# Rows of the FFT input in partition blocks of 32 and 20 instead of 8 and 4

## The chip, the cores and the metric

The kernel runs on one core of one Trainium2 chip. A core has a matrix engine (PE, with its weight loads shown as PEld), three engines for elementwise work (DVE, ACT, POOL), an engine that here only issues transfers (SP), and 16 DMA engines that carry the transfers which SP, ACT and POOL issue. The metric is device time in microseconds of one execution; several runs are summed up by their median.

## The reference

The input x has 8 batches of 3008 rows and 256 columns in float32. The kernel computes the real part of a two-dimensional Fourier transform of each batch and feeds the result, row by row, to a gated feed-forward block of width 1536:

```python
X = np.fft.fft(x, axis=1)
X = np.fft.fft(X, axis=2)
h = X.real.reshape(8 * 3008, 256)
g = h @ w_gate
silu = g * (1.0 / (1.0 + np.exp(-g)))
out = (silu * (h @ w_val)) @ w_out
```

## The kernel before, in words

**How the work is laid out.** The transform along a batch's 3008 rows is done with symmetries. Rows are taken in four quarters of R = 752. Pairs of neighbouring rows that rise from the start of each quarter (the code calls them up, one transfer reads all four quarters of some pairs) are added to pairs that fall from each quarter's end (down, one transfer for each quarter). Of the 188 pair positions of a quarter, 128 go to the tile XA, one to a partition, and the other 60 to half of the tile XC, where two batches share the 128 partitions. POOL folds these rows (lines 171 to 197: cross, even, odd, ab, ce, bb) into bf16 coefficients, PE multiplies the coefficients by cosine and sine tables (lines 1368 to 1419), DVE writes the result into the tiles Pt and Qt, and from there on the feed-forward block runs over 24 tiles of about 512 columns, each column standing for two output rows.

**Units.** A tile is worked through in 12 units of 128 hidden channels; the kernel has 288 units. A unit multiplies Pt and Qt by weights Wp, Wq and Wm into the PSUM tiles g and v (line 972). ACT and DVE turn them into silu values and products (lines 1045 to 1186), POOL multiplies the mirrored ones (line 1183), and PE multiplies hp and hm by Wo (line 1236). The table KINDS gives each unit one hexadecimal digit, which says which engine does which step; a digit with bit 1 set saves one matmul and costs two DVE instructions.

**What sets the order.** From the first unit on nothing is issued directly. Every step is recorded by S.add with an engine, an assumed duration, an assumed latency, and a due time (PE's recorded time so far plus SHIFT and BIAS of the tile). S.run then plays the program through and fixes the order on each queue. The loads are recorded in run_loads (line 1297) with an assumed issue time us, a latency lat and a time ring that the transfer holds the DMA queue. The waiting rows for the next tile are recorded at unit 6 of a tile (first_rows16, line 1569) and unit 7 (all_rows, line 1577): the first copies row 0 of Qt to the tile br, the second copies br to all partitions of bc, both on SP's queue. Stores of finished rows (line 1249) are also on SP's queue. SP uses eight completion semaphores in turn, so the ninth transfer waits until the first has landed.

**What stands in front of the units.** Lines 252 to 652 are issued in the order in which they are written. They load batch 0 directly: one transfer for all 128 rising pairs (line 258), four falling ones by fall_a (line 261, 256 KB each, two from ACT's queue and two from SP's), one for the rising pairs of XC0 (line 264), four by fall_c (line 267, 120 KB each). PE places the rising rows in the partition order of the falling ones with the permutations putA and putC (line 435), DVE adds rising and falling rows (lines 444 to 457), and the first Pt, Qt and weights follow. The first unit's first matmul on line 972 starts at 18.86 us. Batch 1 comes next: load_c(1) partly in front of the units (the first C1_EARLY of its transfers) and partly in the planned part, load_a(1) at unit A1_LOAD.

**Blocks.** [...] A rising transfer (up_block) carries one block, all four quarters. A falling transfer (down_set) carries one quarter of all the blocks; its source has the dimensions [blocks, pairs of a block, 512 elements]. m_cols (line 313) works out a partition's row from LA or LC, so tables follow the blocks.

Of the kernel before, what the change touches and what calls it, by code (L numbers as in the profile page):

```python
# [19 lines left out]
def kernel(  # L20
# [8 lines left out]
    nc = tc.nc  # L29
    B, M, D = x.shape  # L30
    Dff = moe_w_gate.shape[1]
    P = 128
# [20 lines left out]
    NCR = GH - P  # L53
# [62 lines left out]
    rrO = XA.rearrange("p a q d -> p (a q d)")[:, 4 * T:4 * T + 4 * GH].rearrange("p (c q n) -> p c q n", c=2, q=2)  # L116
    kfO = EOf.rearrange("p e a d -> p (e a d)")[:, 4 * (P + 1):4 * (P + 1) + GH]

    LA, NA = 8, P // 8
    LC, NC_ = 4, NCR // 4  # L120

    def up_block(b, j, n):
        return rows_at(b, 2 * j - 1, [[2 * D, n], [R * D, 4], [1, 2 * D]])
# [4 lines left out]
    def down_set(b, a, j, L, n):  # L128

        return rows_at(b, R * (a + 1) - 2 * j, [[2 * L * D, n], [-2 * D, L], [1, 2 * D]])  # L130

    JA, JC = P - LA + 1, GH - LC + 1

    C1_EARLY = 6
    C1_ORDER = "uuduuduuduuduumuueuueuece"
    A1_ORDER = "uuuuduuuuduuuuduuuud"

    def load_a(b, q):
        X3 = XA.rearrange("p a q d -> p a (q d)")
        res = ([lambda h=h: q.dma_start(out=X3[LA * h:LA * (h + 1), 0:4, :],  # L140
                                         in_=up_block(b, JA - LA * h, LA)) for h in range(NA)] +
                [lambda a=a: q.dma_start(out=X3[:, 4 + a, :], in_=down_set(b, a, JA, LA, NA)) for a in range(4)])
        return in_order(A1_ORDER, u=res[:NA], d=res[NA:]) if b == 1 else res

    def in_order(order, **todo):
        todo = {k: list(v) for k, v in todo.items()}
        return [todo[k].pop(0) for k in order]

    def load_c(b, q):

        X3 = XC.rearrange("p a q d -> p a (q d)")
        p0 = 64 * (b % 2)
        pm = p0 + NCR
        r = slice(p0, p0 + NCR)
        ups = [lambda h=h: q.dma_start(out=X3[p0 + LC * h:p0 + LC * (h + 1), 0:4, :],
                                       in_=up_block(b, JC - LC * h, LC)) for h in range(NC_)]
        mid = [lambda: q.dma_start(out=XC[pm:pm + 1, 0:4, 1],
                                   in_=rows_at(b, 0, [[R * D, 1], [R * D, 4], [1, D]]))]
        if b != 1:
            return ups + [lambda a=a: q.dma_start(out=X3[r, 4 + a, :], in_=down_set(b, a, JC, LC, NC_))  # L160
                          for a in range(4)] + mid

        def down(a, k):
            q.dma_start(out=XC[0:NCR, 4 + a, 0] if k else XC[r, 4 + a, 0],
                        in_=rows_at(b, R * (a + 1) - 2 * JC + k, [[2 * LC * D, NC_], [-2 * D, LC], [1, D]]))

        downs = [[lambda a=a, k=k: down(a, k) for a in range(4)] for k in range(2)]
        return in_order(C1_ORDER, u=ups, d=downs[0], e=downs[1], m=mid,
                        c=[lambda: q.dma_start(out=XC[0:NCR, 0:4, 1], in_=XC[r, 0:4, 0])])
# [377 lines left out]
    loads_c1 = load_c(1, q)  # L547
    for load in loads_c1[:C1_EARLY]:
        load()
# [133 lines left out]
    def rows(r0, n, step):  # L683
# [5 lines left out]
    C1_AT = 12  # L689
    A1_AT = 20  # L690
    C2_AT = 39
    A1_LOAD = 8
    ROW_1 = 12
    ROW_2 = 24
    ROW_3 = 35
# [46 lines left out]
    )  # L742
    BIAS = {(t, k): v for t, row in enumerate(BIAS_ROWS) for k, v in zip(SHIFT, row)}
    ES_BUFS = 2
# [175 lines left out]
    def pool_us(n):  # L920
# [6 lines left out]
    ROW_PE = {ROW_1: 1, ROW_2: 2, ROW_3: 3}  # L927
    KINDS = (
        "wwwwwwwwwwww",
        "06ww20001013",  # L930
        "031303160011",
        "000010312133",
        "010210112012",
        "10110b103133",
        "001601031052",
        "300171700001",
        "331213005030",
        "010271031001",
        "34130b310300",
        "01b300700101",  # L940
        "21312101b300",
        "001371310011",
        "32120011b212",
        "10130b135030",
        "000135003170",
        "033170001011",
        "213b21011200",
        "103b10319610",
        "4030b13300b0",
        "616404563200",  # L950
        "143034169230",
        "706150233313",
    )

    def whole(u):
# [328 lines left out]
    lo = C2_AT  # L1284
    for b in range(2, B, 2):
        u = slot[(b, 0)] - 1
        spread(("C", b), 12, lo, (lo + u) // 2)
        spread(("A", b), 12, (lo + u) // 2 + 1, u)
        lo = min(u + 26, slot[(b + 1, 0)] - 2)
# [5 lines left out]
    loads = []  # L1295

    def run_loads(n):
        for what, k, fn in loads[:n]:
            up = k < (NA if what[0] == "A" else NC_)
            r, w, us, ring = [], [((what[0],), k)], 0.4 if up else 0.62, 0.57 if up or what[0] == "C" else 1.14  # L1300
            if what == ("A", 1):
                r = [(("C",), C1_ORDER.rindex("u"))]
                us, ring = (0.42, 0.75) if A1_ORDER[k] == "u" else (0.75, 1.1)
            if what == ("C", 1):
                us, ring = (0.48, 0.75) if C1_ORDER[k] == "u" else (0.95, 1.0)
                if C1_ORDER[k] == "c":
                    r = [(("C",), j) for j, o in enumerate(C1_ORDER) if o == "u"]
            S.add("SP", us, fn, r=r, w=w, after=[(("A",), "pre" if A1_ORDER[k] == "d" else "preW")] if what == ("A", 1) else [],
                  lat=2.5, ring=ring)
        del loads[:n]  # L1310

    FOLD = (("X", "F"), ("F", "E"), ("F", "O"), ("EO", "A"), ("A", "CE"), ("EO", "BB"))
# [112 lines left out]
    for b, part in jobs[1:]:  # L1425
        for eo in range(2):
            u = slot[(b, part)] + eo
# [149 lines left out]
    def all_rows(t):  # L1577
        w = row_width(t)

        def fn():  # L1580
            bc[t] = bcp.tile([P, T], BF16, name="bc")
            nc.sync.dma_start(out=bc[t][:, :w], in_=T_["br", t][0:P:8, :w].unsqueeze(1).to_broadcast([16, 8, w]))
        return fn

    def row_op(t):
        w = width(t)
        kr = (("g", ("bc", t)), 0)

        def product():
            T_[kr] = psG.tile([P, T], F32, name="g")  # L1590
            nc.tensor.matmul(T_[kr][:, :w], sel, pq_tiles(t)[1][:, :w], start=True, stop=True)

        def copy():
            bc[t] = bcp.tile([P, T], BF16, name="bc")
            nc.scalar.copy(bc[t][:, :w], T_[kr][:, :w])  # L1595

        S.add("PE", pe_us(w), product, r=[(("pq", t), "Q")], w=[kr], new=[kr[0]])
        S.add("ACT", act_us(w), copy, r=[kr], w=[(("bc", t), 0)], new=[("bc", t)])
# [4 lines left out]
    S.hold("st", 0)  # L1603
    for k in range(C1_EARLY):
        S.add("DMA", 0.01, lambda: None, w=[(("C",), k)], lat=2.0)
# [11 lines left out]
    for i, u in enumerate(units):  # L1617
        t, f = u
        S.tile = t
        for op in before.pop(i, ()):  # L1620
            op()
        if i == 1:
            loads.extend((("C", 1), k, fn) for k, fn in enumerate(loads_c1) if k >= C1_EARLY)
        if i == A1_LOAD:
            loads[0:0] = ((("A", 1), k, fn) for k, fn in enumerate(load_a(1, nc.sync)))
        run_loads(LOADS if i < 20 else LOADS_LATER)
        if i in ROW_PE:
            row_op(ROW_PE[i])
        for j, k in enumerate((i - ROW_GAP, i)[::-1]):
            tr, fr = divmod(k, nF)  # L1630
            if k >= 0 and fr == 6 and 2 < tr < nT - 1:
                if j:
                    S.add("SP", 0.55, all_rows(tr + 1), r=[(("br", tr + 1), 0)], w=[(("bc", tr + 1), 0)], new=[("bc", tr + 1)], lat=4.5, shift="ROW")
                else:
                    S.add("SP", 0.55, first_rows16(tr + 1), r=[(("pq", tr + 1), "Q")], w=[(("br", tr + 1), 0)], new=[("br", tr + 1)], lat=3.6, shift="ROW")
        if i == RESCALE:
            state["scaled"] = True
            S.add("ACT", 1.3, lambda: nc.scalar.activation(Wm[:, 1], Wm[:, 1], AF.Copy, scale=-0.5),
                  r=[(("Wm",), (fc, 1)) for fc in range(3)], w=[(("Wm",), 1)])
        if i == 2:  # L1640
            S.add("POOL", 1.06, lambda: nc.gpsimd.dma_start(out=Wo, in_=moe_w_out.rearrange("(f p) d -> p f d", p=P)),
                  w=[(("Wo",), 0)], lat=12.0)
        part_a(u)
        if owork:
            owork.run(4)
        if i + 1 < len(units) and seeded(units[i + 1]):
            seed_op(units[i + 1])
        if prev is not None:
            part_b(prev)
            if prev[1] == nF - 1:  # L1650
                owork = OWork(prev[0])
            if owork:
                owork.run(4)
        for what, j in fold_at.get(i, ()):
            fold_step(what, j, i)
        for what in act_at.pop(i, ()):
            load_next(what)
        if i in spread_at:
            spread_op(spread_at[i])
        if i in job_at:  # L1660
            transform_op(*job_at[i])
        prev = u
# [35 lines left out]
```

## Time and profile before

Three runs took 598.28, 599.33 and 600.06 us. The profiled execution took 600.4 us, of which the page's span, from the first to the last instruction, is 598.6 us; its granted clock is 0.999.

| engine | busy us | share of the span |
|---|---|---|
| PE | 587.0 | 98% |
| DVE | 570.3 | 95% |
| ACT | 557.4 | 93% |
| POOL | 527.8 | 88% |

The loads of x by kind, from the list of DMA issues: 30 falling XA transfers of 256 KB and 112 rising ones of 64 KB on SP's queue, 28 falling XC transfers of 120 KB and 105 rising ones of 32 KB, 8 falling half ones of 60 KB for batch 1, two falling XA transfers on ACT's queue, and the two large rising transfers of batch 0.

A time of the span that PE stands idle is lost only if nothing later gives it back; other engines' idle time costs nothing by itself. A window of the profile gives each engine's busy time in a stretch, the share of the 16 DMA engines that was busy (1.00 is all sixteen; transfers that overlap on an engine can lift it a little above), and the rate that they moved.

### The profile page before, as it was taken

Reading aid. Unit: us, or ns where it says so; the run is one execution under the profiler, and the core shown is the slowest. Engines: PE = TensorE matmul, PEld = TensorE weight load, DVE = VectorE, ACT = ScalarE, POOL = GpSimd, SP = SyncE. Lnnn points to the kernel's source line nnn. Section 1 sums busy time; section 2 is a strip of 40 time slices with the busy share of each in tenths; the row PEclk is TensorE's granted clock in tenths of the full one; section 3 lists DMA queues with packets and bytes.
Section 4 is the critical chain, followed back from the end, with each engine's and each line's share of the span. In section 5 each row is a group of like instructions: output and inputs, shape, how many; then the busy total and the mean of one; then the engine's idle time right before and its main releaser. Section 6 shows DMA issues by size and latency. Waiting matters only on the chain.

```text
span 598.6 us, 12468 instructions
## 1 busy us (share of the span) xinstructions
PE 587.0 (98%) x3953; PEld 389.2 (65%) x4012; DVE 570.3 (95%) x1064; ACT 557.4 (93%) x1080; POOL 527.8 (88%) x486
## 2 busy tenths in 40 slices
PE   7999999999999999999999999999999999999997
PEld 5456666666666666666666666666666666666686
DVE  8989999999999999999999999999999999999993
ACT  8778989989998999999999999999999999999995
POOL 8977999999899999998999998897986868687772
PEclk9999999999999999999999999999999999999999
DMA  9956347454715523454127122046221202111212
GB/s 247 150 110 115 109 121 141 132 140 117 178 46 107 136 70 113 123 129 138 57 55 166 46 62 82 19 115 161 63 64 37 65 19 80 48 46 53 60 54 81
DMA packets 51082, 57.65 MB, mean 96 GB/s; under 512 B 7283, under 2 KB 38439, under 8 KB 51017
## 3 DMA queue, kind: packets, MB, share of 16 engines
q1 hardware_dynamic: 47433, 53.91, 35.2%
q0 software_dynamic: 3216, 2.36, 2.8%
q8 instruction: 31, 0.51, 0.4%
q10 hardware_dynamic: 368, 0.59, 0.3%
q14 instruction: 34, 0.28, 0.2%
HBM read 29.43 MB, written 24.65 MB: 90 GB/s over the span
## 4 chain that ended last, share of the span: by engine, by line
PE 71%; ACT 8%; DMA 6%; DVE 4%; POOL 3%; issue 3%; SPq 1%; ACTq 0%; POOLq 0%; DVEq 0%
PE o L1236 30%; PE g L972 19%; PE v L972 16%; DMA XA<-in_x_dram 5%; ACT sv L1159 2%; PE o L1394 2%; PE g L1394 2%; ACT v L1045 2%; ACT es L1107 1%; POOL hm L1183 1%; DVE sv L1175 1%; ACT sp L1084 1%; DVE hp L1186 1%; ACT sp L1156 1%; ACT ev L1243 1%
## 5 line engine op out<-in xcount | busy, mean ns | idle before, releaser
L1183 POOL TENSOR_TENSOR hm<-sv 128x1024 bf16<-128x1024 f32 (+2 forms) x137 | 254.7, 1862 | 44.1 <-ACT sv L1159 17.7
L1175 DVE SCALAR_TENSOR_TENSOR sv<-es,v 128x512 f32<-128x512 f32 (+2 forms) x262 | 173.6, 668 | 5.4 <-PE v L972 2.8
L1236 PE MATMUL o<-Wo,hm 128*128 128x256 bf16 (+1 forms) x1128 | 163.6, 273 | 0.3
L1236 PE MATMUL o<-Wo,hp 128*128 128x256 bf16 (+1 forms) x1104 | 159.7, 273 | 0.2
L1186 DVE TENSOR_TENSOR hp<-sp,v 128x512 bf16<-128x512 f32 (+2 forms) x233 | 154.2, 668 | 2.8 <-PE v L972 2.0
L1236 PEld LDWEIGHTS <-hm 128*128 128x128 bf16 (+2 forms) x1140 | 111.8, 98 | 57.9 <-issue 2.5
L1236 PEld LDWEIGHTS <-hp 128*128 128x128 bf16 (+2 forms) x1140 | 111.9, 98 | 55.8 <-issue 0.9
L1159 ACT ACTIVATE sv<-g 128x512 f32<-128x512 f32 (+2 forms) x179 | 116.7, 671 | 4.6 <-PE g L972 2.3
L1084 ACT ACTIVATE sp<-g 128x512 f32<-128x512 f32 (+2 forms) x179 | 110.5, 621 | 4.1 <-PE g L972 2.7
L972 PE MATMUL v<-Pt,Wp 128*128 128x512 bf16 (+2 forms) x288 | 105.4, 375 | 1.8 <-DVE hp L1186 0.5
L972 PE MATMUL g<-Pt,Wp 128*128 128x512 bf16 (+2 forms) x280 | 104.4, 374 | 0.9 <-ACT sv L1159 0.7
L1045 ACT ACTIVATE v<-bc,w 128x512 f32<-128x512 bf16 (+2 forms) x146 | 104.6, 717 | 0.4
L1109 DVE SCALAR_TENSOR_TENSOR es<-bc,w,v 128x512 f32<-128x512 bf16 (+2 forms) x128 | 92.6, 731 | 2.4 <-ACT bc L1595 0.8
L1107 ACT ACTIVATE es<-v 128x512 f32<-128x512 f32 (+2 forms) x146 | 90.0, 618 | 3.8 <-PE g L972 1.0
L972 PE MATMUL g<-Qt,Wq 128*128 128x512 bf16 (+2 forms) x247 | 90.5, 374 | 0.4
L972 PEld LDWEIGHTS <-Wp 128*128 128x128 bf16 x576 | 56.3, 98 | 27.8 <-DVE Wp L505 0.7
L972 PE MATMUL g<-Qt,Wm 128*128 128x512 bf16 (+2 forms) x186 | 69.8, 375 | 0.2
L1088 DVE SCALAR_TENSOR_TENSOR sg<-bc,w,g 128x512 f32<-128x512 bf16 (+2 forms) x95 | 68.4, 723 | 1.4 <-PE g L972 0.7
L1159 ACT ACTIVATE sv<-sg 128x512 f32<-128x512 f32 (+2 forms) x95 | 65.1, 692 | 0.2 <-DVE sg L1152 0.2
L1152 DVE SCALAR_TENSOR_TENSOR sg<-sg,g 128x512 f32<-128x512 f32 (+2 forms) x95 | 62.9, 662 | 1.5 <-PE g L972 0.8
L1156 ACT ACTIVATE sp<-g 128x512 f32<-128x512 f32 (+2 forms) x95 | 57.7, 608 | 5.5 <-DVE sg L1152 5.3
L972 PE MATMUL v<-Qt,Wm 128*128 128x512 bf16 (+2 forms) x159 | 59.4, 374 | 0.8 <-ACT es L1107 0.4
(218 smaller groups left out, 759.1 us busy)
## 6 DMA issues: line engine op xcount, KB each, us to landing
out_dram<-ev SPq DMA_DIRECT2D x96, 128.0 KB
XA<-in_x_dram SPq DMA_DIRECT2D x30, 256.0 KB
XA<-in_x_dram SPq DMA_DIRECT2D x112, 64.0 KB
XC<-in_x_dram SPq DMA_DIRECT2D x28, 120.0 KB
XC<-in_x_dram SPq DMA_DIRECT2D x105, 32.0 KB
bc<-br SPq DMA_DIRECT2D x19, 128.0 KB
St<-Fc SPq DMA_DIRECT2D x12, 128.5 KB
out_dram<-ev SPq DMA_DIRECT2D x12, 120.0 KB
```

The source lines that it names most:

```text
L972: nc.tensor.matmul(ps[:, :n], Wt[:, gv, fs], src[:, :n], start=start, stop=stop, skip_group_check=True)
L1045: nc.scalar.activation(T_[kv][:, :w], bc[t][:, :w], AF.Copy, scale=w0[:, 1, f:f + 1])
L1084: nc.scalar.activation(sp_to()[:, :w], T_[kg][:, :w], AF.Silu)
L1088: nc.vector.scalar_tensor_tensor(T_[keg][:, :w], bc[t][:, :w], w0[:, 0, f:f + 1], T_[kg][:, :w], op0=Alu.mult, op1=Alu.add)
L1107: nc.scalar.activation(T_[kes][:, :w], T_[kv][:, :w], AF.Copy, scale=2.0 if on_pool(u) > 1 else 1.0)
L1109: nc.vector.scalar_tensor_tensor(T_[kes][:, :w], bc[t][:, :w], w0[:, 1, f:f + 1], T_[kv][:, :w], op0=Alu.mult, op1=Alu.add)
L1156: nc.scalar.activation(sp_to()[:, :wp], T_[kg][:, :wp], AF.Silu)
L1159: nc.scalar.activation(sv()[:, f % 2, w - 1::-1, 1], T_[kgm if by_dve else kg][:, :w], AF.Silu)
L1175: nc.vector.scalar_tensor_tensor(sv()[:, f % 2, w - 1::-1, 0], T_[kes][:, :w], 2.0, T_[kv][:, :w], op0=Alu.mult, op1=Alu.subtract)
L1183: nc.gpsimd.tensor_tensor(hts_(t)[1][:, f - 1:f + 1, :w], sv()[:, :, :w, 1], sv()[:, :, :w, 0], op=Alu.mult)
L1186: nc.vector.tensor_tensor(hts_(t)[0][:, f, :wp], T_[ksp][:, :wp], T_[kv][:, :wp], op=Alu.mult)
L1236: nc.tensor.matmul(st["ps"][:n, j, :], hts[t][minus][:, f, c:c + n], Wo[:, f, :], start=(f == 0), stop=(f == nF - 1))
```

## The change

The blocks become 32 pairs in XA (4 blocks) and 20 in XC (3 blocks). A rising XA transfer then has 32 rows and 256 KB, and there are 4 to a batch instead of 16; a rising XC transfer has 20 rows and 160 KB, and there are 3 instead of 15. The falling transfers keep their number and size; their source changes from 16 blocks of 8 to 4 blocks of 32 (XA) and from 15 of 4 to 3 of 20 (XC). This holds for batch 0 in front of the units too, since fall_a and fall_c call down_set with LA, NA, LC and NC_. Orders and times of the loads, the kinds of the units and the biases of the due times are set anew.

```diff
-    LA, NA = 8, P // 8
-    LC, NC_ = 4, NCR // 4
+    LA, NA = 32, P // 32
+    LC, NC_ = 20, NCR // 20
...
-    C1_EARLY = 6
-    C1_ORDER = "uuduuduuduuduumuueuueuece"
-    A1_ORDER = "uuuuduuuuduuuuduuuud"
+    C1_EARLY = 5
+    C1_ORDER = "uuuddddmeceee"
+    A1_ORDER = "uuuudddd"
...
-    A1_LOAD = 8
+    A1_LOAD = (6, 8)
...
+    BIAS_ROWS = (
...
-        "06ww20001013",
-        "031303160011",
+        "02ww20502010",
+        "021013330011",
...
         for what, k, fn in loads[:n]:
-            up = k < (NA if what[0] == "A" else NC_)
-            r, w, us, ring = [], [((what[0],), k)], 0.4 if up else 0.62, 0.57 if up or what[0] == "C" else 1.14
+            r, w, us, ring = [], [((what[0],), k)], 0.6, 0.75 if what[0] == "C" else 1.14
             if what == ("A", 1):
                 r = [(("C",), C1_ORDER.rindex("u"))]
-                us, ring = (0.42, 0.75) if A1_ORDER[k] == "u" else (0.75, 1.1)
+                us, ring = 0.62, 1.1
             if what == ("C", 1):
-                us, ring = (0.48, 0.75) if C1_ORDER[k] == "u" else (0.95, 1.0)
+                us, ring = (0.6, 0.8) if C1_ORDER[k] == "u" else (0.92, 0.8)
...
-                  lat=2.5, ring=ring)
+                  lat=4.0, ring=ring)
...
-        if i == A1_LOAD:
-            loads[0:0] = ((("A", 1), k, fn) for k, fn in enumerate(load_a(1, nc.sync)))
+        if i in A1_LOAD:
+            lo = 4 * A1_LOAD.index(i)
+            loads[0:0] = ((("A", 1), k, fn) for k, fn in enumerate(load_a(1, nc.sync)) if lo <= k < lo + 4)
```

The two functions that give a transfer its source, unchanged but called with the new numbers:

```python
def up_block(b, j, n):
    return rows_at(b, 2 * j - 1, [[2 * D, n], [R * D, 4], [1, 2 * D]])

def down_set(b, a, j, L, n):
    return rows_at(b, R * (a + 1) - 2 * j, [[2 * L * D, n], [-2 * D, L], [1, 2 * D]])
```

More of the change, by code (lines that the diff above doesn't have):

```diff
@@ L741 @@
         (25.4, -5.2, -1.45, -3.3, -3.05, 7.35, -3.65, 2.4, 0.6, -2.3, 21.2, -2, -6.05, -1.9, 13.3, 7.65, -18.55),
+    )
+    BIAS_ROWS = (
[24 rows of a table added]
     )
@@ L929 @@
         "wwwwwwwwwwww",
-        "06ww20001013",
-        "031303160011",
[L932 to L937, printed above, removed]
+        "02ww20502010",
+        "021013330011",
+        "301130110133",
+        "010210112103",
+        "01110b103133",
+        "001201131052",
+        "001071600001",
+        "331213050030",
         "010271031001",
         "34130b310300",
-        "01b300700101",
-        "21312101b300",
+        "01b340700101",
+        "21312110b200",
         "001371310011",
         "32120011b212",
[L944 to L949, printed above, removed]
+        "10130b130001",
+        "031035003170",
+        "053370040011",
+        "203b21011210",
+        "103b10219610",
+        "0130b03300b0",
         "616404563200",
         "143034169230",
-        "706150233313",
+        "704121733313",
     )
```

24 rows, old and new, of the table BIAS_ROWS are left out of this document.

## The prediction

> **What bounds the kernel now.** I read the page first, then the windows by stage. The page says that PE carries the chain and is busy nearly throughout.
>
> ```profile
> span 598.6 us, 12468 instructions
> PE 71%; ACT 8%; DMA 6%; DVE 4%; POOL 3%; issue 3%; SPq 1%; ACTq 0%; POOLq 0%; DVEq 0%
> ```
>
> The windows (each engine's busy time, PEclk, DMA share, GB/s) say where PE is not busy.
>
> ```profile
> 0.00:19.00 19.00, 15.91 (x104) 10.00 (x106) 16.56 (x69) 14.73 (x25) 17.43 (x40) 1.00 0.89 220
> 19.00:64.00 45.00, 44.53 (x276) 25.52 (x278) 41.51 (x76) 36.47 (x71) 37.22 (x50) 1.00 0.69 124
> 64.00:110.00 46.00, 44.16 (x299) 29.17 (x301) 43.40 (x82) 41.20 (x79) 45.76 (x45) 1.00 0.54 132
> 110.00:560.00 450.00, 447.21 (x2997) 296.77 (x3046) 440.23 (x784) 433.82 (x832) 404.85 (x338) 1.00 0.34 87
> 560.00:598.60 38.60, 35.22 (x283) 27.74 (x282) 28.59 (x58) 31.16 (x74) 22.57 (x17) 0.99 0.23 68
> ```
>
> Between 19 and 560 us PE idles 0.47 + 1.84 + 2.79 = 5.1 us in all. So neither faster loads nor a better plan has more than that to win there, and whatever holds up the first unit moves the end by as much, since a full PE can't catch up. The stage before 19 us has the busiest DMA engines, 0.89 of all sixteen. There the loads of batch 0 feed DVE and PE directly (timeline of PE, then of DVE).
>
> ```profile
> 11.27 1.95 PE L435 MATMUL o<-XC,putC 128*128 128x512 f32 x4 [0.99 <-DMA XC<-in_x_dram]
> 18.86 0.57 PE L972 MATMUL g<-Pt,Wp 128*128 128x480 bf16 x2
> 7.80 0.68 DVE L444 TENSOR_TENSOR FA<-g,XA 128x510 f32<-128x510 f32 x1
> 10.30 0.42 DVE L448 TENSOR_TENSOR FA<-v,XA 128x256 f32<-128x256 f32 x1
> 12.40 0.42 DVE L448 TENSOR_TENSOR FC<-o,XC 128x256 f32<-128x256 f32 x1 [0.44 <-PE o L435]
> 13.66 0.42 DVE L448 TENSOR_TENSOR FC<-o,XC 128x256 f32<-128x256 f32 x1
> ```
>
> PE waits 0.99 us for XC's rising rows. The falling rows are used at 7.80 us (the first XA quarter) to 13.66 us (the last XC ones), and from there 5.20 us of chained work lead to the first matmul of unit 0 at 18.86 us.
>
> **Part 1: how many DMA engines a transfer gets.** Three steady windows and those of batch 0, of the same view:
>
> ```profile
> 2.00:6.00 4.00, 3.15 (x41) 2.97 (x39) 3.97 (x19) 3.93 (x10) 3.81 (x9) 1.00 1.00 327
> 6.00:9.00 3.00, 2.85 (x7) 1.44 (x8) 2.83 (x8) 2.80 (x4) 2.75 (x6) 1.00 1.06 291
> 13.00:16.00 3.00, 2.95 (x17) 1.65 (x17) 2.70 (x9) 1.74 (x4) 2.92 (x6) 1.00 1.21 199
> 224.00:226.00 2.00, 2.00 (x15) 1.31 (x14) 2.00 (x5) 2.00 (x5) 1.92 (x3) 1.00 0.23 70
> 311.00:313.00 2.00, 2.00 (x16) 1.35 (x14) 2.00 (x4) 2.00 (x5) 2.00 (x2) 1.00 0.52 74
> 325.00:327.00 2.00, 1.95 (x15) 1.32 (x14) 2.00 (x5) 2.00 (x5) 2.00 (x2) 1.00 1.05 248
> ```
>
> What SP had issued at these times (SP's timeline):
>
> ```profile
> 308.33 5.81 SPq L140 DMA_DIRECT2D XA<-in_x_dram  x12
> 320.97 2.48 SPq L142 DMA_DIRECT2D XA<-in_x_dram  x4
> ```
>
> At 311 to 313 us rising XA transfers of 8 rows are under way, several behind each other, and 0.52 of sixteen engines, 8.3, are busy. At 224 to 226 us rising XC transfers of 4 rows run, with 0.23 or 3.7 engines. At 325 to 327 us the falling XA ones with 16 blocks run, with all sixteen. So the engines follow the outermost count, 8, 4 and 16, and with twelve rising transfers queued the share stays near 8: the next one goes to the same engines. A rising XA transfer after has 32 rows and can use sixteen. A falling one has an outermost count of 4 (XA) or 3 (XC) in the source, but 128 or 60 partitions in the destination. No transfer in this trace has sides that differ in this way (16 blocks and 128 rows both allow sixteen). I take the smaller side, on the assumption that an engine's share has to be a whole stretch of the outer dimension of both. So I forecast four engines for a falling XA transfer and three for an XC one, the same ones each time.
>
> By the Trainium skill, DMA: Bandwidth & Descriptors, section Why a DMA increments its semaphore by 16 and not by 1, the engine count is the largest number up to 16 that divides the outermost counts of both sides, on the lowest-numbered engines. The windows agree for 8, 4 and 16; for unequal sides no run here shows it. By it the counts are 4 and 3 and the sum is the one below; with the destination's count alone it would be rival A's.
>
> **Part 2: batch 0's loads, on the path.** Bytes on each of the three busiest engines: rising XA 1024 KB / 16 = 65.5 kB, rising XC 512 KB / 16 = 32.8 kB, falling XA 4 x 256 KB / 4 = 262 kB, falling XC 4 x 120 KB / 3 = 164 kB. That is 524 kB against 194.6 before (3113 kB over sixteen). Rates of one engine: 327 / 16 = 20.4 kB/us in the first window, 291 / 16 = 18.2 where batch 0's falling rows come in, 248 / 16 = 15.5 for falling rows later on. I take 20.4 for the rising and, as fewer engines then compete, 19.3 for the falling (between the two rows of batch 0; ends 20.4 and 15.5). Rising: 98.3 / 20.4 = 4.8 us. Falling: 426 / 19.3 = 22.1 us (20.9 to 27.5). The first weights, two transfers of 262 kB that start before XC's rows are in, take turns with them on these engines at 1.3 us each by the 199 GB/s of 13 to 16 us: 2.6 us (0 if they come wholly behind, 4 if a third joins). The first byte moves at 2.0 us, and about 1 us (0.5 to 1) passes from last byte to use: before, 2.0 + 98.3 / 20.4 + 96.3 / 18.2 + 1 = 13.1, against 13.66 seen. After: 2.0 + 4.8 + 22.1 + 2.6 + 1.0 = 32.5 us (28.2 to 39.3). The last addition of XC moves from 13.66 to 32.5, **18.8 us later** (14.5 to 25.6). PE, DVE and ACT stand waiting in program order; nothing else is there to do, so no cover hides it, and the first unit starts at 37.7.
>
> **Part 3: the loads of later batches, beside other work.** Rising rows win: 16 transfers that took from 308.33 to about 321 us become 4 on sixteen engines, 1049 / 327 = 3.2 us. Falling rows lose: 4 x 65.5 / 19.3 = 13.6 us on four engines, where 1049 / 248 = 4.2 us did. Together 17 us as before (12.7 + 4.2), hidden by a batch's (598.6 - 18.9) / 8 = 72 us; XC's go from 30 small transfers and 8 falling ones for two batches to 6 and 8 x 41 / 19.3 = 17 us. POOL's one wait for rows and the bc copy's waits are these:
>
> ```profile
> POOL SDf L178 <- DMA XA<-in_x_dram: 2.1, 1, 2.1
> SPq L1582 <- DMA br<-Qt: 11.7, 9, 2.3
> ```
>
> The 2.1 us of POOL lie at 59 us; gone with them is at most the 1.84 us of PE idle time of 64 to 110. I take -1 (0 to -2.3 with the stage before). What is late next is SP's queue: stores, br and bc now stand behind falling rows on four engines. Stores have three ev buffers at one eviction in some 6 us, so 13.6 us are borne. In the new order br follows directly on four falling XA transfers, with three stores between, at two places; I take +1 us for these (0 to 13, rival C).
>
> **Part 4: SP's instructions and the new plan.** SP issues 168 transfers fewer (629 to 461, by count of the programs), none of which PE waits for: 0, and the cover is SP's own idle time. Pairs of rising and falling rows keep the tables' sizes; m_cols and the permutations have as many instructions as before: 0. One unit less is of the kind that saves a matmul, so PE has one more 512-column matmul:
>
> ```profile
> L972 PE MATMUL g<-Qt,Wq 128*128 128x512 bf16 (+2 forms) x247 | 90.5, 374 | 0.4
> ```
>
> That is +0.4 at most, and DVE has two instructions of some 0.7 us less, off the path. Other kinds only change places. The new due times can win no more than the 2.8 us of idle time of 110 to 560, and may lose as much: 0 (-2.8 to +3).
>
> **Sum**, against the profiled execution's 600.4 us (its span 598.6): +18.8 - 1 + 1 + 0.4 = +19.2, 619.6. The execution lies 1.07 above the median of 599.33, so **618.5 us**.
>
> **The rivals.**
> A, the other side: the destination's count alone decides, so falling rows keep sixteen (or fifteen) engines and batch 0 loads as before; or each transfer takes another set of engines, which comes to the same. For it: the windows show no transfer with unequal sides. Against it: an engine would then have to start within a block, and against other sets the share near 8 under twelve queued transfers. The rising rows would be faster and at best the 1.84 + 0.47 us of idle time to 110 go: 599.3 - 1 + 0.4 = 598.7 (597 to 601 with the plan's bounds), not slower. It decides from the point where the rate between 6 and 13 us stays near 280 GB/s.
> B, half as much: few engines run faster than any row shows, and the weights come behind. With 27 kB/us, a third above the best row, part 2 gives 2.0 + 4.8 + 15.8 + 0.5 = 23.1, so +9.4, and with the 2.3 us won back 600.4 + 9.4 - 2.3 + 0.4 - 1.07 = 606.8. For it: all rows have other engines at work beside. Against it: the rates of the rows go down, not up, from 20.4.
> C, the waiting rows: besides part 2, br waits behind four falling transfers for 13.6 us and bc with it. A unit is (598.6 - 18.9) / 288 = 2.0 us; bc is due with the next tile's first seed, five units or 10 us after br is asked for, and the planner counts 3.6 + 4.5 us for the two, so some 3 us of slack stand against 10 of delay: up to 6.5 us at each of two places, 618.5 + 12 = 630.5. Falling rows at 15.5 kB/us end there too (+5.4 in part 2, +3 later). Against it: S.run spaces them by a modelled 1.1 us a transfer, and three stores in between wait for ACT.
> D, the planned part is a good deal better or worse than before for reasons that no view shows: 595, or 640.
>
> **How the numbers follow.** The forecast, 607 to 627: 0.66. C, 627 to 640: 0.10. B, 602 to 607: 0.08. A, 597 to 602: 0.13. D: 0.03. The predicted time is the forecast's, 618. The range of 605 to 632 holds the forecast, the upper half of B and half of C, some 0.77, and rounds to 0.8; its lower end leaves A out. Three tenths of a percent, 1.8 us, is what a measurement of this kernel tells from no change. Slower: forecast, C, B and half of D, 0.86. Same: half of A, 0.06. Faster: 0.08.
>
> **What would show it.** Part 1: between 8 and 28 us a DMA share near 0.25 and some 80 GB/s instead of 1.06 and 291; the same with falling XA rows in a later batch. Part 2: DVE's second addition on line 448 with FC near 32 us and the first matmul of line 972 near 38. Part 3: rising XA rows in about 3 us; PE idle by less than 3 us from there to the end of each stage; if C, waits of line 1045 or 1109 for bc. Part 4: PE with one matmul more. The prediction is wrong if the share stays at 1 in batch 0's load (A), or if the first unit starts near 38 and the end moves by much less, since then a full PE did catch up.

## The result and the profile after

The changed kernel takes 627.31 us (median of four runs, 626.90 to 630.67) where the kernel before, run beside it, takes 599.39 us: 1.048 times as long, 95% interval 1.0441 to 1.0519. The forecast was 618 us with a range of 605 to 632. So the direction is right, and the loss of 28 us is half as large again as the 19 foretold. From span to span it is 625.5 - 598.6 = 26.9 us.

First two lines of the page, with span and busy times, then three rows of the waits of the whole run (engine, what it waits for, total us, times, longest).

```profile
span 625.5 us, 12307 instructions
PE 597.8 (96%) x4013; PEld 391.4 (63%) x4013; DVE 570.8 (91%) x1063; ACT 555.2 (89%) x1079; POOL 526.3 (84%) x485
PE o L435 <- DMA XC<-in_x_dram: 12.1, 1, 12.1
PE v L490 <- DVE EOf L457: 4.2, 1, 4.2
POOL SDf L178 <- DMA out_dram<-ev: 6.1, 2, 3.9
```

PE waits 12.1 us once for XC's rows and 4.2 us once for the second half of them. The last row is of two other places, near 291 and 440 us, and returns below.

The windows of batch 0's load (busy time of PE, PEld, DVE, ACT, POOL; PEclk, the granted clock; DMA share; GB/s), then DVE's and PE's timeline of the same stretch:

```profile
12.00:16.00 4.00, 0.00 (x0) 0.00 (x0) 1.43 (x4) 0.62 (x1) 2.03 (x3) 0.81 0.28 85
16.00:20.00 4.00, 0.00 (x0) 0.00 (x0) 0.41 (x1) 0.00 (x0) 1.49 (x2) 0.50 0.88 163
20.00:24.00 4.00, 1.83 (x2) 0.84 (x3) 1.99 (x8) 1.91 (x5) 1.18 (x2) 0.50 0.37 83
32.00:36.00 4.00, 1.90 (x7) 0.88 (x8) 2.94 (x12) 1.37 (x3) 1.07 (x4) 0.50 0.24 55
```

```profile
12.56 0.69 DVE L444 TENSOR_TENSOR FA<-g,XA 128x510 f32<-128x510 f32 x1 [4.62 <-DMA XA<-in_x_dram]
19.59 0.43 DVE L448 TENSOR_TENSOR FA<-g,XA 128x256 f32<-128x256 f32 x1 [5.60 <-DMA XA<-in_x_dram]
27.10 0.42 DVE L448 TENSOR_TENSOR FC<-o,XC 128x256 f32<-128x256 f32 x1 [5.04 <-DMA XC<-in_x_dram]
32.69 0.42 DVE L448 TENSOR_TENSOR FC<-o,XC 128x256 f32<-128x256 f32 x1 [4.25 <-DMA XC<-in_x_dram]
```

```profile
22.17 3.75 PE L435 MATMUL o<-XC,putC 128*128 128x512 f32 x4 [12.07 <-DMA XC<-in_x_dram]
34.10 0.50 PE L490 MATMUL v<-Tab,EOf 128*128 128x378 bf16 x1 [4.24 <-DVE EOf L457]
39.47 0.57 PE L998 MATMUL g<-Pt,Wp 128*128 128x480 bf16 x2
```

Between 12 and 16 us 0.28 of the DMA engines are busy, 4.5 of sixteen, where batch 0's load had kept all of them busy before. The rows' two queues (SP's and ACT's) make 0.20 and 72 GB/s of it; the rest is a weight transfer of POOL's queue. Between 8 and 10 us the rows have 0.26 and 93 GB/s. From 16 to 20 us the weights run on the other engines as well, so the share says nothing about the rows there. The last XC addition is at 32.69 us, the first unit at 39.47, 20.6 us later than before. From the addition to the unit it is 6.78 us instead of 5.20. In this stretch the granted clock is 0.50, and the matmul of line 490 takes 0.50 us, where it took 0.33 in the kernel before. The four matmuls that place XC's rows are slowed too (3.75 us instead of 1.95), but they lie ahead of the last addition, which waits for rows.

Behind the first unit another 6.3 us are lost. Windows where PE is not full, with one where it still is:

```profile
280.00:330.00 50.00, 48.41 (x330) 31.82 (x329) 47.06 (x86) 46.74 (x91) 45.46 (x40) 1.00 0.25 75
435.00:440.00 5.00, 5.00 (x38) 3.35 (x37) 5.00 (x15) 4.89 (x11) 2.68 (x4) 1.00 0.27 101
440.00:445.00 5.00, 3.33 (x24) 2.17 (x23) 2.79 (x9) 1.97 (x4) 3.35 (x3) 1.00 0.24 60
445.00:450.00 5.00, 3.27 (x15) 1.80 (x15) 2.69 (x6) 3.65 (x7) 5.00 (x4) 0.80 0.38 110
```

The chain from 425 to 455 us names the wait there (start, us, what):

```profile
426.31 0.71 SPq L142
427.06 14.43 DMA XA<-in_x_dram
441.65 0.04 POOL SDf L178
444.17 1.85 POOL hm L1209
446.04 0.65 ACT sv L1185
446.73 0.38 PE g L998
448.25 0.85 PE o L1262 x4
450.39 0.85 PE o L1262 x4
451.82 0.44 PE o L1262 x4
```

SP issues the last falling XA transfer of the last batch at 426.31 us, and its rows are there 14.43 us after the issue ended. Up to 429 us other transfers, the rising ones among them, keep the engines busy (1.05 of them from 426 to 428 us); from then on the falling rows go on to 0.26 to 0.27 of the engines. POOL's fold on line 178 stands in its queue and waits; the product hm behind it, ACT and PE follow. The waits above name a store for this (3.9 us), the chain names XA's rows; with the later falling rows read from many blocks (below) the wait is 0.3 us, so it is the rows. PE idles 1.67 + 1.73 us in the two windows, one gap of 3.40 us, and from 448 to 451.8 us its matmuls take 0.85 us for four instead of 0.44. At 291 us the same fold waits 2.2 us, and by POOL's sv and DVE's es PE loses 1.6 us.

That closes the account. With the last stage left out, PE idles 6.2 us from the first unit on, where the kernel before idled some 2; 3.4 us at half the clock cost some 1.7 (an estimate: half of them), and one matmul more some 0.4.

### The profile page after: what moved, and what is told of

The parts are those of the page before. It is cut to its first block, busy times and chain, and to the rows that moved or that the text cites. A ratio compares the mean times of both kernels' runs of the same rounds, so it can differ in the third digit from the quotient of the medians.

```text
span 625.5 us, 12307 instructions
## 1 busy us (share of the span) xinstructions
PE 597.8 (96%) x4013; PEld 391.4 (63%) x4013; DVE 570.8 (91%) x1063; ACT 555.2 (89%) x1079; POOL 526.3 (84%) x485
## 4 chain that ended last, share of the span: by engine, by line
PE 69%; DMA 13%; ACT 5%; DVE 4%; SPq 4%; issue 3%; POOL 2%; POOLq 0%; ACTq 0%; DVEq 0%
PE o L1262 30%; PE g L998 20%; PE v L998 15%; DMA out_dram<-ev 6%; DMA XC<-in_x_dram 5%; DMA XA<-in_x_dram 2%; SPq L267 1%; ACT sv L1185 1%; DVE sv L1201 1%; PE g L1419 1%; PE o L1419 1%; SPq L160 1%; POOL SDf L178 1%; DVE hp L1212 1%; DVE es L1135 1%
## 5 line engine op out<-in xcount | busy, mean ns | idle before, releaser
L1262 PEld LDWEIGHTS <-hp 128*128 128x128 bf16 (+2 forms) x1140 | 111.8, 98 | 54.4 <-issue 0.5
L1185 ACT ACTIVATE sv<-g 128x512 f32<-128x512 f32 (+2 forms) x180 | 119.1, 674 | 8.2 <-POOL hm L1209 4.4
L998 PE MATMUL g<-Pt,Wp 128*128 128x512 bf16 (+2 forms) x288 | 107.7, 376 | 4.0 <-ACT sv L1185 3.8
L998 PE MATMUL g<-Qt,Wq 128*128 128x512 bf16 (+2 forms) x288 | 105.6, 376 | 0.0
L998 PE MATMUL g<-Qt,Wm 128*128 128x512 bf16 (+2 forms) x194 | 73.1, 377 | 0.0
L1269 ACT COPY ev<-o 128x512 f32<-128x512 f32 x89 | 55.0, 618 | 8.1 <-PE o L1262 4.4
```

The costliest lines, as they stand in the source:

```text
L998: nc.tensor.matmul(ps[:, :n], Wt[:, gv, fs], src[:, :n], start=start, stop=stop, skip_group_check=True)
L1185: nc.scalar.activation(sv()[:, f % 2, w - 1::-1, 1], T_[kgm if by_dve else kg][:, :w], AF.Silu)
L1262: nc.tensor.matmul(st["ps"][:n, j, :], hts[t][minus][:, f, c:c + n], Wo[:, f, :], start=(f == 0), stop=(f == nF - 1))
```

## The experiments

Each time stands against the kernel before, which took 599.2 to 599.6 us beside these runs. Two theories stood at the start: few DMA engines on the falling rows make the loss (nearly all in batch 0), or the new plan and the later loads do.

**Batch 0 alone.** The kernel before, with batch 0's falling rows read in few blocks:

```diff
-        eng.dma_start(out=XA3[:, 4 + a, :], in_=down_set(0, a, JA, LA, NA))
+        eng.dma_start(out=XA3[:, 4 + a, :], in_=down_set(0, a, P - 31, 32, 4))
...
-        in_=down_set(0, 3 - 2 * hi - a, JC, LC, NC_))
+        in_=down_set(0, 3 - 2 * hi - a, GH - 19, 20, 3))
```

> The kernel before, with one part of the change alone: batch 0's four falling XA transfers read 4 blocks of 32 pairs and its four falling XC ones 3 blocks of 20; its rising rows, the tables and all later loads stay. Left out: batch 0's falling rows then lie in the wrong partitions, so its part of the output isn't the reference's; the work is the same. Theory T (few DMA engines on batch 0's falling rows make most of the loss): DMA share near 0.25 and some 80 GB/s from 16 to 28 us, DVE's second addition on line 448 with FC near 32.7 us, first matmul of line 972 near 39.5, the end 18 to 22 us later than before, 617 to 621. Rival P (the loss is from the later loads and the new plan, which this kernel has not): 599 to 602.

615.88 us, ratio 1.027 (1.0247 to 1.0293): +16.3.

```profile
30.71 0.42 DVE L448 TENSOR_TENSOR FC<-o,XC 128x256 f32<-128x256 f32 x1 [2.28 <-DMA XC<-in_x_dram]
37.03 0.57 PE L972 MATMUL g<-Pt,Wp 128*128 128x480 bf16 x2
84.00:130.00 46.00, 45.79 (x316) 30.98 (x319) 45.40 (x87) 42.31 (x82) 45.77 (x45) 1.00 0.51 130
```

Nothing but the block count of eight transfers has changed, so the blocks of these eight are the cause of a late start, and the share of busy engines above shows by what. The first unit is 37.03 - 18.86 = 18.2 us late, the end 16.3. The difference lies where the kernel before idled 1.84 us between 64 and 110: in the stretch that answers to it PE is full now. The end is 1 us below what theory T gave. The first unit, too, comes sooner than the 39.5 expected, and 2.4 us sooner than the changed kernel's; what else makes that one late was not traced.

**Batch 0 put back, and all put back.** Two kernels from the changed one. The first undoes the above in it, the second also reads the later falling rows from 16 and 15 blocks (the same numbers in load_a and load_c).

> The changed kernel, with that one part undone: batch 0's falling transfers read 16 blocks of 8 pairs (XA) and 15 of 4 (XC) again. Left out: those rows lie in the wrong partitions, so batch 0's output isn't the reference's. Theory T: the first matmul of line 998 is back near 19 us, and the end comes earlier by those 20.6 us: 606.7 (605 to 609); the some 6 us that are left come later. Rival P: 625 to 628. Rival L (the late start is also what upsets the later work, so nothing is left without it): 599 to 602.

> The changed kernel with all falling transfers of all batches reading 16 blocks of 8 (XA) and 15 of 4 (XC), so that only the wide rising transfers and the new plan are left of the change. Left out: the falling rows lie in the wrong partitions, so the output isn't the reference's. Theory T (the 6 us left are POOL's wait for later falling rows on four engines): 599 to 602, the wait of POOL's line 178 before 442 us gone. Rival Q (the new plan or the wide rising transfers cost the 6 us): 605 to 608, the same as with batch 0's falling rows alone put back.

The first took 618.88 us, ratio 1.032 (1.0294 to 1.0345); the second 601.99 us, ratio 1.0043 (1.0024 to 1.0061). The second lies where theory T had it (599 to 602). For the first T had 606.7, and fell, as did P and L: with batch 0 mended and a first unit at 18.90 us, the later falling rows cost 618.9 - 602.0 = 16.9 us, not 6. The first kernel's window, waits and POOL timeline show where:

```profile
40.00:84.00 44.00, 38.19 (x219) 23.10 (x221) 34.83 (x59) 27.44 (x53) 34.26 (x36) 0.92 0.37 110
POOL SDf L178 <- DMA XA<-in_x_dram: 6.2, 2, 4.5
PE g L998 <- ACT sp L1110: 5.3, 2, 3.0
45.60 2.35 POOL L178 TENSOR_TENSOR SDf<-XC 128x1020 f32<-128x1020 f32 x1 [4.52 <-DMA XA<-in_x_dram]
62.56 2.35 POOL L178 TENSOR_TENSOR SDf<-XA 128x1020 f32<-128x1020 f32 x1 [1.73 <-DMA XA<-in_x_dram]
```

POOL's folds of batch 1 wait for rows, XC's for 4.5 us up to 45.6 and XA's for 1.7 us up to 62.6, and PE is idle for 5.8 us between 40 and 84. In the changed kernel the units start 20 us later, but batch 1's loads only 6 to 12 us: SP issues the falling XC rows from 27.0 us on instead of 20.8, the falling XA rows from 54.4 instead of 42.5. There PE is full from 45 to 84 us and the folds wait 0.3 us. So the two losses overlap. What stays in the second kernel, 2.6 us, is of the plan and the wide rising transfers together, which no run parts; its PE waits 3.6 us for the later column blocks of the weights, which the kernel before did not:

```profile
PE o L1467 <- DMA XA<-in_moe_w_gate_dram: 2.5, 1, 2.5
PE o L1467 <- DMA XA<-in_moe_w_val_dram: 1.1, 2, 0.8
```

**The other order.** If the losses overlap, putting back the later rows alone must win little more than the 6 us seen.

> The changed kernel with the falling transfers of all batches but batch 0 reading 16 blocks of 8 (XA) and 15 of 4 (XC); batch 0's stay at 4 and 3 blocks. Left out: those later rows lie in the wrong partitions, so the output isn't the reference's. With batch 0's put back alone the end was 618.9, with all put back 602.0. Theory O (the losses overlap: a late start gives batch 1's loads a head start, so that its slow falling rows, which cost PE some 9 us by 80 us when the units start on time, cost nothing then): no POOL wait of line 178 before 442 us, first matmul of line 998 at 37 to 39.5 us, and 616 to 620. Rival S (the losses add: 627.3 less the 16.9 us of the later ones): 609 to 612.

618.77 us, ratio 1.0324 (1.0309 to 1.034): theory O, with the first unit at 39.90 us, a little later than it had. PE is then full, but for gaps of some 0.05 to 0.1 us where the trace lacks a matmul's record:

```profile
430.00:480.00 50.00, 49.73 (x337) 33.16 (x342) 48.73 (x90) 48.00 (x93) 42.55 (x36) 1.00 0.20 59
```

The changed kernel's loss is then, in medians: 2.6 us of plan and wide rising rows, 618.8 - 602.0 = 16.8 of batch 0's falling rows, 627.3 - 618.8 = 8.5 of the later ones. In the other order the last two are 8.4 and 16.9.

**The clock.** Matmuls that nothing reads keep PE busy ahead of XC's rows, in the changed kernel and then in the one with the later rows put back.

```diff
-    warm(8)
+    warm(160)
...
+    for _ in range(48):
+        nc.tensor.matmul(acc[1][0][:, 3 * P:4 * P], sel, sel, start=True, stop=True, skip_group_check=True)
     cross_halves(FC[:, 1], XC0, psC, 1)
```

> The changed kernel with PE kept busy by matmuls that nothing reads: 160 instead of 8 of 128 columns ahead of XC's placement, and 48 more into unused columns ahead of the second half of XC. Theory H (TensorE's granted clock of 0.50 after PE's idle 12 us stretches the chain from the last XC addition to the first unit from 5.20 to 6.78 us): granted clock 1.00 from 22 to 40 us, the 128x377 matmul of line 490 at 0.32 instead of 0.52 us, the first matmul of line 998 near 37.9 us, and the end 1.6 us earlier, 625.7. Rival: the clock is not what sets the chain (DVE, ACT or the rows are): 39.5 us and 627, unchanged.

> Both edits at once: the changed kernel with all falling rows but batch 0's read from 16 and 15 blocks, and PE kept busy ahead of XC's rows by 160 and 48 matmuls that nothing reads. Left out: the later falling rows lie in the wrong partitions, so the output isn't the reference's. Without the busy PE it took 618.8, with the first matmul of line 998 at 39.90 us, and PE is full from 40 us to the end. In the changed kernel itself the busy PE brought the first unit 1.3 us forward and the end not at all. Theory H1 (the lost 1.3 us were taken back by waits on later falling rows; where these are gone the full PE carries them to the end): first unit near 38.3, end 616.9 to 617.8. Rival H2 (what the clock costs in front of the units is given back in any case): 618.5 to 619.2.

In the changed kernel the first unit moved from 39.47 to 38.13 us, with the last XC addition at 33.37 and the granted clock at 1.00 from 30 us on, so the chain behind it took 4.76 us. The matmul of line 490 took 0.33 us instead of 0.50:

```profile
34.77 0.33 PE L490 MATMUL v<-Tab,EOf 128*128 128x378 bf16 x1 [1.44 <-DVE EOf L457]
38.13 0.57 PE L1000 MATMUL g<-Pt,Wp 128*128 128x480 bf16 x2
```

The end did not come earlier: the profiled run took 627.36 us, with a span of 625.6 where the kernel without it had 625.5, and three other runs 630.4 to 630.5, which makes the median 630.46. The changed kernel has the same two times, three runs near 627 and one at 630.67; what parts them is not known. With the later rows put back the end did move: 616.36 us against 618.77, the first unit at 37.30 instead of 39.90, half a us more than theory H1 had. So the clock costs 2.4 us of the late start, and in the changed kernel what it costs does not show at the end, where waits for later rows remain. In which of them the 1.3 us go was not pinned down.

**Blocks of 16.** If time follows the bytes on the busiest engine, eight engines should lose little. The kernel before with `LA, NA = 16, P // 16` and the list of loads shortened to match; then batch 0's falling XA rows alone from 8 blocks, and the later ones alone, both with the planned order kept.

> The kernel before with blocks of 16 pairs in XA alone (8 blocks; XC stays at 4), in all batches: rising XA transfers of 16 rows and 128 KB, falling ones from 8 blocks. Theory T (engines follow the smaller outermost count, time follows the bytes on the busiest engine): falling XA rows on 8 engines add 65.5 kB to each of these in batch 0; at the 21 kB/us of the kernel whose batch 0 alone had few blocks (328 kB more in 15.6 us) that is 3.1 us, the first matmul of line 972 near 22 us, and the end 601.5 to 605. Rival W (any number of blocks under sixteen costs as the smallest does): first unit beyond 27 us and 608 or more. Rival N (eight engines are enough, as other transfers fill the rest): 599 to 601.

> The kernel before with batch 0's four falling XA transfers alone read from 8 blocks of 16; all else, the planned order too, stays. Left out: those rows lie in the wrong partitions, so batch 0's output isn't the reference's. In the kernel with blocks of 16 in XA throughout the first matmul of line 972 started at 25.8 us (6.9 us late) and the end was 16.1 us late. Theory M (the late start is batch 0's and 2.6 us of it are won back as in the kernel whose batch 0 alone had few blocks; the other 9 us are made after it): first unit near 25.8, end 602.5 to 605. Rival R (the late start alone upsets the units after it): 608 or more.

> The kernel before with the falling XA transfers of all later batches alone read from 8 blocks of 16; batch 0, the rising rows, XC and the planned order stay. Left out: those rows lie in the wrong partitions, so the output isn't the reference's. Theory M1 (the 9 us that blocks of 16 lost after the first unit come from the order that the planner made anew for 8 rising transfers instead of 16, not from the slower rows): 598.5 to 601. Rival M2 (falling rows on eight engines, 2 us each, come too late for POOL or hold up stores): 604 to 609.

Blocks of 16 took 615.91 us, ratio 1.0281 (1.0266 to 1.0297), eleven more than theory T allowed, and the time that rival W had; W's first unit beyond 27 us did not come, though, so no theory held whole. Its first unit:

```profile
16.43 3.71 PE L435 MATMUL o<-XC,putC 128*128 128x512 f32 x4 [5.98 <-DMA XC<-in_x_dram]
20.19 0.42 DVE L448 TENSOR_TENSOR FC<-o,XC 128x256 f32<-128x256 f32 x1 [0.32 <-PE o L435]
25.79 0.57 PE L972 MATMUL g<-Pt,Wp 128*128 128x480 bf16 x2
```

The placement of XC's rows starts 16.43 - 11.27 = 5.2 us late, which is more than the 3.1 us of bytes, likely since the first weights, issued from 8.2 us on, now move before XC's rows are in; no run parts this. Then the half clock (0.50 from 14 to 20 us) makes it 3.71 instead of 1.95 us long. Together that is the 6.9 us of the first unit. The two parts: batch 0 alone 605.02 us, ratio 1.0093 (1.0075 to 1.0111), first unit at 25.32; the later rows alone 604.06 us, ratio 1.0075 (1.0049 to 1.0101), with runs from 598.67 to 606.58. So +5.8 and +4.8 of the +16.6; the rest, 6, belongs to the rising rows of 16, to the order that the planner made anew for them, or to the two losses meeting. Theory M and rival M2 hold at their edges, M1 falls: eight blocks for the later rows are too few already, if by little.

**The plan.** The changed blocks under the plan of before (kinds, due times, assumed load times), the later falling rows alone in the order of before, and the changed kernel with one number of its plan nearer to the trace (`ring = 2.7` for falling XA rows).

> The kernel before with the change's blocks (32 and 20) and the orders of the shorter lists of loads, but its own kinds of units, due times and assumed load times. Theory (blocks make the loss, the plan little): 622 to 633, with the first matmul of line 972 at 37 to 39.5 us. Rival P1 (the changed plan made a good part of the loss): 615 to 620. Rival P2 (the changed plan already won back a good part): 636 or more.

> The kernel before with the falling transfers of all later batches read from 4 blocks of 32 (XA) and 3 of 20 (XC); batch 0 and the planned order stay. Left out: those rows lie in the wrong partitions, so the output isn't the reference's. It is the part of the change that the kernel with batch 0's few blocks alone left out. In the changed kernel the later falling rows cost 16.9 us with a start on time and 8.5 us with the late start. Theory (rows that land late for POOL's folds and stores that wait behind them, whatever the plan): 611 to 622, with a wait of POOL's line 178 for rows near 45 to 65 us. Rival (the order before has the slack for them): 599 to 604.

> The changed kernel with one number of its plan changed: a falling XA transfer from batch 2 on is taken to hold the DMA queue for 2.7 us, as in the trace, instead of 1.14. Theory F (POOL's folds stand in its queue ahead of the rows since the plan counts them too early, and the end of the late loss is that): POOL's waits of line 178 after 280 us shorten from 6.1 us to under 2, and the end comes 3 to 6 us earlier, 621 to 624. Rival G (the wait only moves, as the order around it is made anew): 626 to 630.

The blocks alone: 634.57 us, ratio 1.0596 (1.0574 to 1.0617), between the theory's range and rival P2's. So the changed plan does not cost; it wins 634.6 - 627.3 = 7.3 us on these rows. The later falling rows alone in the order of before: 640.94 us, ratio 1.0688 (1.0669 to 1.0707), +41.7 and more than anyone's range. Its waits:

```profile
POOL SDf L178 <- DMA out_dram<-ev: 15.9, 2, 10.2
DVE es L1109 <- DMA bc<-br: 15.3, 2, 8.8
PE v L972 <- DVE es L1109: 13.8, 3, 8.6
```

Here the waiting row of the next tile stands behind the falling rows and stops PE, as rival C had it, for up to 8.6 us and 13.8 in all; the folds of line 178 wait too. In the changed kernel no engine waits for the transfer of bc. The single number of the plan made things worse: 635.92 us, ratio 1.0614 (1.0598 to 1.063). POOL's waits for rows are nearly gone, as theory F had it, but PE is idle elsewhere, for some 3 us between 480 and 580 alone, where it is full in the changed kernel (of the 3.5 that the window lacks, 0.8 are short gaps where the trace lacks a matmul's record):

```profile
POOL SDf L178 <- DMA XA<-in_x_dram: 0.4, 1, 0.4
480.00:580.00 100.00, 96.53 (x629) 62.06 (x639) 94.51 (x167) 92.18 (x178) 72.69 (x52) 1.00 0.17 49
```

The time is in neither theory's range. A planned order changes as a whole when one duration does, so this run doesn't price the wait; the kernel with the later rows put back, which keeps the order, does.

## Why the prediction was right or wrong

**Part 1, right.** Falling XA rows kept 0.26 of the engines busy, against 0.25 foretold: by their two queues from 8 to 10 us, and alone from 436 to 438, with 98 GB/s. Falling XC rows alone had 0.20, or 3.1 engines, and 73 GB/s (148 to 150 us). A transfer whose source has 4 blocks and whose destination has 128 rows uses some four engines, and one with 3 blocks three, so the smaller side decides; rival A is out. The rule of the Trainium skill (DMA: Bandwidth & Descriptors, Why a DMA increments its semaphore by 16 and not by 1), by which the engine count has to divide both outermost counts, agrees with these shares. The rate of an engine was 93 / 4 = 23 kB/us between 8 and 10 us and 72 / 4 = 18 from 12 to 16, with weights beside, against 19.3 taken. Later rows reached 98 / 4 = 24.5 alone, so the rate does go up with few engines, near rival B's 27; the prediction held the opposite against B. B stayed away all the same, since batch 0's rows, which it speaks of, ran at 18 to 23.

**Part 2, right up to the rows, short behind them.** The last XC addition came at 32.69 us where 32.5 was worked out. That it is so near is in part luck: rows that run alone go faster than 19.3 kB/us, so whatever shares the engines with them took more than the 2.6 us put down for weights. The step that failed is the 5.20 us of chained work taken as fixed: it took 6.78, as the granted clock was 0.50. That nothing covers the delay was also too simple: of the 20.85 us between the first units of the two kernels that differ in batch 0 alone (19.05 and 39.90), 16.8 reach the end. Part of what came back, in the kernel that starts on time, is the 3.6 us wait for weights.

**Part 3, the step that made the error.** "-1 for POOL's wait" and "+1 for br and bc", so nothing for the later rows: they cost 8.5 us. The loads are as short as worked out or shorter (four falling XA transfers, 1049 kB at 98 GB/s, are 10.7 us, where 13.6 was taken), and less than a batch's 72, but a batch's time isn't the slack: POOL's fold is put into its queue for the time at which the planner thinks that rows are there, and it holds up the hm products behind it. The prediction looked for the damage in SP's queue (stores, br, bc). That mechanism is real, since in the order of before (+41.7 in all) PE waits 13.8 us behind it, but the changed order avoids it. Where POOL's 2.1 us wait was to vanish, a 3.9 us one came.

**Part 4, nearly right.** Loads and plan together cost 2.6 us with fast falling rows, inside the bounds of -2.8 to +3. PE has one weight load more (4013 against 4012), so one matmul more; DVE, ACT and POOL have one instruction less each, where two less were foretold for DVE, off the path either way. A plan worth about 0 fits only the fast rows; against slow ones it is worth 7.3. The lower bound was misread: the trace of before has 3953 matmuls to 4012 weight loads, and nearly all of the 2.8 us that PE seems idle from 110 to 560 us are gaps of under 0.1 us at missing records. From 19 to 560 us some 2 us were idle, not 5.1, so there was less to win than the prediction thought.

**The sum.** Foretold 18.8 - 1 + 1 + 0.4 = 19.2; by the runs 16.8 + 8.5 + 2.6 = 27.9. The term of batch 0 came out smaller, as two errors partly cancel (the clock's 2.4 us, and 4 us that come back); the miss is the later rows. The end lies at the border of the forecast's case and C's, by neither's reason. The direction and the first 17 us follow from the mechanism foretold; that the whole lies within 605 to 632 owes something to a width that was put there for C.

## What to carry to other kernels

Here a transfer was as parallel as the smaller of its two outermost counts, with 4 and 3 blocks against 128 and 60 rows: before merging or reshaping transfers to save their number, look at both sides, and at the DMA share while nothing else runs. The cost of a slow load is not its length against a stage's length but the place where its consumer was queued: in POOL's queue one fold that waited 3.9 us made all that stood behind it late, and PE lost 3.4 us. And two delays need not add: to price one, undo it both alone and with the other undone.

## What the runs showed of the hardware that was not expected

An idle PE is paid for twice. After PE stopped at 10.1 us its granted clock was still 1.00 from 12 to 14 us and 0.50 from 16, and stayed there for some 6 us of work after 22.17. At 29.9 us PE stopped again, and some 1.7 us later the clock fell once more:

```profile
12.00:14.00 2.00, 0.00 (x0) 0.00 (x0) 1.43 (x4) 0.00 (x0) 0.05 (x1) 1.00 0.28 89
14.00:16.00 2.00, 0.00 (x0) 0.00 (x0) 0.00 (x0) 0.62 (x1) 1.98 (x3) 0.63 0.27 81
26.00:28.00 2.00, 2.00 (x8) 0.90 (x6) 0.85 (x2) 0.00 (x0) 0.39 (x1) 0.50 0.65 156
28.00:30.00 2.00, 1.72 (x8) 0.50 (x6) 0.42 (x1) 0.00 (x0) 0.00 (x0) 0.96 1.02 142
30.00:32.00 2.00, 0.00 (x0) 0.00 (x0) 0.00 (x0) 0.00 (x0) 0.00 (x0) 0.89 0.53 137
```

This second fall is the one that stretches the chain behind the last XC addition, and the 48 matmuls of the experiment fill the gap ahead of it. Near 446 us, after 3.4 us of idle time, PE worked on at 1.00 from 446.7 to 448 us and had 0.50 only from 448 to 450.

The Trainium skill (TensorE: Matmul & The Clock Gate, Part 1: The HAM clock gate) has the clock halve after an idle window of about 3.4 us and return after as long a busy one; the first fall, 4.4 us after PE stopped, agrees with these rows. The return came some 6 us after work began, which fits if a whole busy window has to pass, as the section has the windows run on freely. The other two falls do not fit a wholly idle window: ahead of one PE had been idle for 1.7 us, ahead of the other it had been at work again for 1.3 us. By these rows a stretch that is idle in part was enough.
